# An FNet and GEGLU kernel: a row tile's products a and b taken as 512 and 384 columns instead of 448 and 448

## The chip, the cores and the metric

The kernel runs on one core of a Trainium2 chip. The metric is the device time of one execution in microseconds, as a median over runs. TensorE (PE in the profile; PEld is its loading of weights) multiplies into PSUM, a memory of eight banks of 128 partitions x 512 float32 values. VectorE (DVE) and ScalarE (ACT) read those banks and work on SBUF. GpSimd (POOL) adds some tiles and issues DMAs, and SyncE (SP) issues most DMAs. Each engine works through its own queue in order, and waits for the others by semaphores.

## What is computed

`x` has 2048 rows of 448 values. After a layer norm the kernel takes a two-dimensional Fourier transform of it, real part only, as matrix products, and multiplies it by a gate from a GEGLU block:

```python
a = jnp.einsum("bsd,ed->bse", x, dft_hid_re)
b = jnp.einsum("bsd,ed->bse", x, dft_hid_im)
y = jnp.einsum("ts,bse->bte", dft_seq_re, a) - jnp.einsum("ts,bse->bte", dft_seq_im, b)

def _B_ref(x, w_gate, w_up, w_down):
    return (_gelu(x @ w_gate) * (x @ w_up)) @ w_down

xn = _layernorm(x, axis=-1)
s = _A_ref(xn, A_dft_seq_re, A_dft_seq_im, A_dft_hid_re, A_dft_hid_im)
g = _silu(_B_ref(xn, B_w_gate, B_w_up, B_w_down))
return x + s * g
```

All matrices are float32.

## The kernel before

Each factor of a product is split into a high part, rounded by a ScalarE copy to the type that TensorE takes, and a low part, the rest, by a VectorE subtraction (`split`, L148 to L150: the two lines show as L149 and L150 wherever it is used). A product is then high x high + high x low + low x high.

The program has three stages one after the other. First come the layer norm, the transposes and the GEGLU block (to about 396 us). Then comes the stage of a and b (396 to 477 us), which the change touches. Last comes the transform along the sequence (477 us to the end), which uses a and b. The order of every instruction is the order in which the code is written; nothing is rescheduled. The framework adds the waits, and it treats the accesses of two engines to one PSUM tile as ordered.

**The stage of a and b** is the loop at L1213 over 16 row tiles k of 128 rows, in the order 0 to 13, 15, 14. In a row tile `hid_mm` (L1095) makes two products, each of 11 matmuls (4 high x high, 3 high x low, 4 low x high) into one PSUM bank: `ab{k}_0` is a, 448 columns, and `ab{k}_1` is b, 448 columns. The rows of x in high and low part (`xth`, `xtl`) are the weights, and the two transform matrices along the hidden axis are the moving operand. Those are prepared by `e_split` (L955) in four tiles of 128 contraction rows, the matrices side by side, 896 columns.

Two kinds of row tile follow.
- Row tiles 10 and 15 (`KP`) go to `hid_plain` (L1109). ScalarE and VectorE split a (L149, L150), then minus b (L1112, L1113).
- The other 14 go to `hid_sums` (L1118). ScalarE copies a into pieces 0 and 7 of a buffer `f`, 224 columns each (L1123), and minus b into pieces 2 and 6 (L1124). VectorE makes four more pieces of them (L1129 to L1132). A row tile later `hid_split` (L1136) splits the seven pieces (ScalarE L1141, VectorE L1144). From row tile 2 on there are two buffers `f` in turn, so L1123 of a row tile waits for L1144 of the tile two before it. From k = 11 the split stands right behind the sums.

In row tiles 2 to 5 ScalarE also does a SiLU (L1239). Ahead of the first three row tiles and between them a few products of the block before (`po`, L422) are sent.

**The stage behind it** runs over units of one row tile each (`seven`, L1282): seven products in seven banks, each a matmul of 448 columns with the high part of the factors (L1289) and one of 224 columns with the low part (L1292). `sum_c` (VectorE, L1194 and L1195) and `prep_c` (ScalarE L149, then VectorE L150) prepare the factors of a unit. Those of unit 0 are prepared in row tile 10, and those of units 1 to 3 right behind the loop: `prep_c(1)`, then the sums of row tile 14, then `prep_c(2)` and `prep_c(3)` (L1253 to L1256). The place that `prep_c(1)` writes held the hidden matrices, so it waits for the last matmul of row tile 14. The banks of the seven products are those of the last row tiles of the stage before, in turn: 11, 12, 13, 15 and 14.

Of the kernel before, what the change touches and what calls it, by code (L numbers as in the profile page):

```python
# [8 lines left out]
F32 = mybir.dt.float32  # L9
FR = mybir.dt.float32r  # L10
AF = mybir.ActivationFunctionType
ALU = mybir.AluOpType
# [3 lines left out]
D = 448  # L16
# [11 lines left out]
HD = D // 2  # L28
# [31 lines left out]
def fnet_geglu(ctx: ExitStack, tc: tile.TileContext, xw, ca, ct, cp, et, wss, wd, out):  # L60
# [15 lines left out]
    nc = tc.nc  # L76
# [24 lines left out]
    a_ws = sb.tile([P, 7680], FR, name="w")  # L101
# [12 lines left out]
    def part(t, off, a, b):  # L114
        v = t[:, off : off + a * b].rearrange("p (a b) -> p a b", a=a)
        return v
# [4 lines left out]
    xth = [part(a_x[c], 0, 4, 512) for c in range(NC)]  # L121
    xtl = [part(a_x[c], 2048, 4, 512) for c in range(NC)]
# [5 lines left out]
    def bank(i, name):  # L128
        return psum.tile([P, 512], F32, name=name, tag=f"b{i}")
# [3 lines left out]
    def in_turn(kind, name):  # L133

        first, n = {"mm": (0, 4), "tp": (4, 2), "o": (6, 2), "x": (0, 5), "po": (5, 3), "all": (0, 8)}[kind]
        turns[kind] += 1
        return bank(first + turns[kind] % n, name)
# [10 lines left out]
    def split(h, l, src):  # L148
        nc.scalar.activation(h, src, AF.Copy)  # L149
        nc.vector.tensor_sub(l, src, h)  # L150
# [400 lines left out]
    with tc.manual_schedule():  # L551
# [356 lines left out]
        h, l = [[v[:, n] for n in range(4)] for v in (xth[1], xtl[1])]  # L908
# [21 lines left out]
        e_raw, e_at = {}, {}  # L930
# [24 lines left out]
        def e_split(b):  # L955

            r = e_raw[b]
            if b == 3:
                e_at[b] = []
                for i in range(2):  # L960
                    h, q = a_ws[:, 3584 + i * D :][:, :D], r[:, i * D : (i + 1) * D]
                    nc.scalar.activation(h, q, AF.Copy)
                    nc.vector.tensor_sub(h[64:], q[64:], h[64:].bitcast(F32))
                    e_at[b].append(h)
                return
            v = (a_ws[:, 1792:3584], a_d[1], a_ws[:, :1792])[b]
            split(v[:, : 2 * D], v[:, 2 * D :], r)
            e_at[b] = [v[:, i * D : (i + 1) * D] for i in range(4)]

        for n, (p, f) in enumerate(blocks):  # L970
            g = f // 2
# [9 lines left out]
            if p == 0:  # L981
# [12 lines left out]
                if f in (8, 11):  # L994

                    k = slice(0, 4, 3) if f == 8 else slice(1, 3)
                    for i in range(2):
                        v, w = [u[:, i * 2048 :][:, :2048] for u in (sp, a_x[1].bitcast(F32))]
                        v, w = [u.rearrange("p (k d) -> p k d", k=4)[:, k] for u in (v, w)]
                        nc.sync.dma_start(v, w)  # L1000
            elif f == 2:
                q = None
                for v, w in zip(prep, t1_steps[6][1:]):
                    v.append(w)
                dn[3] = then(send, *t1_steps[7][:2])
            elif f == 3:

                late = then(late[0], t1_steps[7][2]), late[1]
                v = sb.tile([P, 8 * D], F32, name="gacc2", tag="u1")
                for c in range(2):  # L1010
                    gacc[2 + c] = part(v, c * 4 * D, 4, D)
                    nc.sync.dma_start(v[:, c * 4 * D :][:, : 4 * D], gsp[c])
                v = sb.tile([P, 4096], FR, name="w2", tag="u0")
                slots.append((v[:, :WH], v[:, WH : WH + WL]))
            elif f == NF - 3:
                e_load(2)
            elif f == NF - 2:
                dn[1] = dn[3] = then(send, send)
                prep[2].append(lambda: e_split(2))
                prep[2].extend([lambda b=b: e_load(b) for b in (1, 0, 3)])  # L1020
            elif f == NF - 1:
                prep[1].append(lambda: e_split(0))
                prep[2].extend([lambda: e_split(3), lambda: e_split(1)])
                dn = [then(send, send), send, nop, nop]
# [56 lines left out]
        def f_at(k):  # L1081
            if k == 1:
                return a_t[:, : 8 * HD]
            if k % 2 == 0 and k < 13:
                return a_r[:, : 8 * HD]
            if "d0" not in new:
                new["d0"] = sb.tile([P, 4 * D], F32, name="f1", tag="d0")
            return new["d0"]

        TS, ab, behind = {}, {}, []  # L1090
# [4 lines left out]
        def hid_mm(k):  # L1095
            c, kk = divmod(k, 4)
            sl = slice(kk * P, (kk + 1) * P)
            ps = []
            for r in range(2):
                p = in_turn("x" if k < 2 else "all", f"ab{k}_{r}")  # L1100
                mm = [(xth[c][:, b, sl], e_at[b][r]) for b in range(4)]
                mm += [(xth[c][:, b, sl], e_at[b][2 + r]) for b in range(3)]
                mm += [(xtl[c][:, b, sl], e_at[b][r]) for b in range(4)]
                for n, (a, b) in enumerate(mm):
                    nc.tensor.matmul(p[:, :D], a, b, start=n == 0, stop=n == len(mm) - 1)  # L1105
                ps.append(p[:, :D])
            return ps

        def hid_plain(k, ps, spots):  # L1109
            split(spots[0][:, :D], spots[0][:, D:], ps[0])  # L1110
            h, l = spots[1][:, :D], spots[1][:, D:]
            nc.scalar.activation(h, ps[1], AF.Copy, scale=-1.0)  # L1112
            nc.vector.scalar_tensor_tensor(  # L1113
                l, ps[1], -1.0, h.bitcast(F32), op0=ALU.mult, op1=ALU.subtract
            )
            ab[k] = [(v[:, :D], v[:, D:]) for v in spots]

        def hid_sums(k, ps):  # L1118


            fs[k] = f_at(k)
            f = fs[k].rearrange("p (i d) -> p i d", d=HD)
            nc.scalar.activation(f[:, 0:8:7], ps[0].rearrange("p (i d) -> p i d", i=2), AF.Copy)  # L1123
            nc.scalar.activation(  # L1124
                f[:, 2:7:4], ps[1].rearrange("p (i d) -> p i d", i=2), AF.Copy, scale=-1.0
            )

            def sums_():
                nc.vector.tensor_sub(f[:, 4], f[:, 7], f[:, 0])  # L1129
                nc.vector.tensor_sub(f[:, 3], f[:, 6], f[:, 7])  # L1130
                nc.vector.tensor_sub(f[:, 5], f[:, 6], f[:, 4])
                nc.vector.tensor_sub(f[:, 1], f[:, 2], f[:, 5])  # L1132

            return sums_
# [77 lines left out]
        nc.sync.dma_start(a_x[1].bitcast(F32), sp)  # L1212
        for k in [*range(14), 15, 14]:  # L1213
            ps = hid_mm(k)
            if k == 0:
                late[0]()
# [6 lines left out]
            if k in KP:  # L1223
                hid_plain(k, ps, [rest(v) for v in ((new["u0"], new["u1"]), a_x[1:3])[k > 10]])
            else:
                hid_sums(k, ps)()
# [9 lines left out]
            if 2 <= k < 6:  # L1236

                c = k - 2
# [13 lines left out]
        load_c(5)  # L1252
        prep_c(1)  # L1253
        sums14 = hid_sums(14, ps)
        prep_c(2)
        prep_c(3)  # L1256
# [87 lines left out]
        for m, (j, k) in enumerate(units):  # L1344
            u = m % UN
            end = j == NK // 2 - 1
            if u == 0:
                ps = {q: bank(banks[i], f"p{q}_{j}") for i, q in enumerate(PRODUCTS)}
            if k in KS:
# [7 lines left out]
                for i in range(8):  # L1357
                    if u != at[i]:
                        continue
                    i, h = divmod(i, 4)  # L1360
                    TS[KX[(j + 1) % 2][i]] = TS[KX[j % 2][i]]
                    n = KX[(j + 1) % 2][i]
                    a, b = [v.rearrange("p (b d) -> p b d", d=D) for v in (TS[n], td[n])]
                    a, b = a[:, PARTS[h]], b[:, PARTS[h]]
# [135 lines left out]
```

## Time and profile before

| | |
|---|---|
| median of 3 runs | 768.38 us (768.17 to 768.41) |
| the profiled execution's own time | 768.08 us |
| its span, first to last instruction | 766.3 us |
| matmuls | 4041, of them 352 in the stage of a and b |
| granted TensorE clock | 0.999 |

Rows of the profile read as: line, engine, operation, out<-in by the program's names (x rows<-row type), count | busy us, mean ns of one | idle us before, and who ended it. Rows of a timeline begin with the start and the duration in us from the span's start, and end, in brackets, with the engine's idle time before the instruction and who ended it. The matmul's own duration (365 ns for 448 columns) holds its way through the array; the next one starts well before it ends, so the time of a step is read from one start to the next.

### The profile page before, as it was taken

The numbers are of one execution on the slowest core, as the hardware profiler recorded it, in microseconds if no ns is written. First come the engines' busy times: TensorE is split into PE (matmuls) and PEld (weight loads), VectorE is DVE, ScalarE is ACT, GpSimd is POOL, SyncE is SP. The second block draws the span as 40 slices with busy tenths as digits, with TensorE's granted clock in tenths as the row PEclk, the third lists the DMA queues.
The fourth block names the chain that finished last, engine by engine and source line by source line (L and its number), as shares of the span: only waits on it lengthen the run. The fifth ranks groups of instructions, "written<-read, shape, count | busy, mean of one in ns | idle before, by whom it ended". The sixth has DMA issues, their size and how long they took to land.

```text
span 766.3 us, 11490 instructions
## 1 busy us (share of the span) xinstructions
PE 760.0 (99%) x4041; PEld 685.6 (89%) x4041; DVE 641.7 (84%) x1087; ACT 351.4 (46%) x499; POOL 122.8 (16%) x162
## 2 busy tenths in 40 slices
PE   9999999999999999999999999999999999999997
PEld 8988888888888888888889999999999999999997
DVE  7987789999989888988876677988889797979786
ACT  5866433444435334343344755544444344444441
POOL 2002332422434224232200000000000000000000
PEclk9999999999999999999999999999999999999999
DMA  8077484949568563738642732869696969788794
GB/s 299 15 223 233 118 246 138 233 154 243 205 142 298 139 207 82 223 79 245 153 184 85 296 165 69 279 224 338 209 352 206 341 213 311 248 279 277 246 324 153
DMA packets 81034, 162.28 MB, mean 212 GB/s; under 512 B 8016, under 2 KB 62800, under 8 KB 79568
## 3 DMA queue, kind: packets, MB, share of 16 engines
q1 hardware_dynamic: 75648, 135.02, 51.5%
q0 software_dynamic: 5184, 26.41, 16.1%
q8 instruction: 32, 0.52, 0.3%
q14 instruction: 26, 0.21, 0.1%
q10 hardware_dynamic: 144, 0.11, 0.0%
HBM read 139.36 MB, written 51.25 MB: 249 GB/s over the span
## 4 chain that ended last, share of the span: by engine, by line
PE 98%; DVE 1%; issue 0%; ACT 0%; DVEq 0%
PE x L444 24%; PE p L1289 21%; PE po L422 18%; PE p L1292 10%; PE ab L1105 9%; PE x L456 4%; PE gu L371 3%; PE gu L592 2%; PE py L1309 1%; PE py L1311 1%; PE py L1310 1%; PE pt L206 1%; PE warm L571 1%; PE pt L649 0%; DVE cc L1384 0%
## 5 line engine op out<-in xcount | busy, mean ns | idle before, releaser
L422 PE MATMUL po<-wd,hs 128*128 128x448 f32 x672 | 152.7, 366 | 0.0
L422 PEld LDWEIGHTS po<-wd,hs 128*128 128x128 f32 x672 | 125.8, 188 | 14.2
L444 PE MATMUL x<-xt,w 128*128 128x512 f32 x432 | 114.1, 391 | 0.0
L444 PEld LDWEIGHTS x<-xt,w 128*128 128x128 f32 x432 | 81.1, 188 | 15.3
L149 ACT ACTIVATE w<-raw 128x896 fp32r<-128x896 f32 (+1 forms) x59 | 53.6, 910 | 61.9 <-DVE raw L1195 22.4
L444 PE MATMUL x<-t,w 128*128 128x512 f32 x276 | 80.8, 391 | 0.0
L433 DVE TENSOR_TENSOR gacc<-gacc,po 128x448 f32<-128x448 f32 x96 | 58.5, 615 | 14.3 <-PE po L422 14.2
L1105 PE MATMUL ab<-w,xt 128*128 128x448 f32 x256 | 68.1, 365 | 0.0
L521 ACT ACTIVATE hs<-tmp 128x512 fp32r<-128x512 f32 x24 | 15.2, 633 | 101.1 <-DVE tmp L519 101.1
L444 PEld LDWEIGHTS x<-t,w 128*128 128x128 f32 x276 | 51.8, 188 | 9.3
L1289 PE MATMUL p<-xt,w 128*128 128x448 f32 x168 | 54.3, 374 | 0.0
L320 POOL TENSOR_TENSOR raw<-raw 128x256 f32<-128x256 f32 x23 | 19.7, 858 | 212.0 <-DMA raw<-wss 158.2
L1334 POOL DMA_DIRECT2D cc<-xw x14 | 12.3, 881 | 252.8 <-DVE raw L1194 96.1
L1105 PEld LDWEIGHTS ab<-w,xt 128*128 128x128 f32 x256 | 48.1, 188 | 3.8
L149 ACT ACTIVATE w<-f 128x896 fp32r<-128x896 f32 (+1 forms) x34 | 30.2, 888 | 41.7 <-DVE f L1195 17.4
L150 DVE TENSOR_TENSOR w<-raw,w 128x896 fp32r<-128x896 f32 (+1 forms) x40 | 41.8, 1046 | 2.0 <-ACT w L149 1.4
L339 ACT ACTIVATE w<-raw 128x768 fp32r<-128x768 f32 x24 | 20.3, 846 | 39.8 <-POOL raw L326 39.8
L1289 PE MATMUL p<-ts_g,w 128*128 128x448 f32 x112 | 36.3, 374 | 0.0
L1289 PE MATMUL p<-ts_u,ts_tmp 128*128 128x448 f32 x112 | 36.3, 374 | 0.0
L1289 PE MATMUL p<-hs,w 128*128 128x448 f32 x112 | 35.5, 374 | 0.0
L1105 PE MATMUL ab<-wd,xt 128*128 128x448 f32 x96 | 35.1, 365 | 0.0
L1289 PEld LDWEIGHTS p<-xt,w 128*128 128x128 f32 x168 | 31.5, 188 | 2.4
(297 smaller groups left out, 1849.6 us busy)
## 6 DMA issues: line engine op xcount, KB each, us to landing
sums<-ca SPq DMA_DIRECT2D x16, 896.0 KB, 8.8
sums<-ca POOLq DMA_DIRECT2D x16, 896.0 KB, 9.8
raw<-ct SPq DMA_DIRECT2D x69, 192.0 KB, 4.2
raw<-wss SPq DMA_DIRECT2D x24, 512.0 KB, 3.8
ts_u<-td SPq DMA_DIRECT2D x24, 448.0 KB, 5.7
ts_g<-td SPq DMA_DIRECT2D x24, 448.0 KB, 6.5
raw<-sums SPq DMA_DIRECT2D x69, 128.0 KB, 4.1
f<-ct SPq DMA_DIRECT2D x39, 192.0 KB, 4.5
```

Source lines behind the costliest of these rows:

```text
L149: nc.scalar.activation(h, src, AF.Copy)
L150: nc.vector.tensor_sub(l, src, h)
L320: eng.tensor_add(r[:, 1:16:14], r[:, 0:14:13], r[:, 9:17:7])
L339: nc.scalar.activation(h[:, :n], src[:, :n], AF.Copy)
L371: nc.tensor.matmul(ps[:, cols], a, xt[:, k, cols], start=n == 0, stop=n == len(mm) - 1)
L422: nc.tensor.matmul(po[:, :D], hs[:, a, kk * P : (kk + 1) * P], wdn[:, b, i], start=n == 0, stop=n == 5,)
L433: nc.vector.tensor_add(ga, ga, po[:, :D])
L444: nc.tensor.matmul(ps, a[i], b[j], start=first and n == 0, stop=n == 2, skip_group_check=True)
L456: nc.tensor.matmul(ps, a[0], x_, start=False, stop=True, skip_group_check=True)
L1105: nc.tensor.matmul(p[:, :D], a, b, start=n == 0, stop=n == len(mm) - 1)
L1289: nc.tensor.matmul(ps[q][:, :D], h, v, start=u % UN == 0, stop=False, skip_group_check=True)
L1292: nc.tensor.matmul(ps[q][:, :HD], l, v[:, :HD], start=False, stop=u % UN == NS - 1, skip_group_check=True,)
```

## The change

The two products of a row tile are cut at another column. a and b stand side by side, 896 columns; the first bank now takes columns 0 to 511 (all of a and the first 64 of b), the second bank the other 384 of b. What reads b reads it in pieces: in `hid_plain` 64 and 384 columns, in `hid_sums` 64, 160 and 224. Lines move by up to three: L1105 becomes L1104, L1124 becomes L1129, L1129 to L1132 become L1132 to L1135, L1141 and L1144 become L1144 and L1147, L1194 and L1195 become L1197 and L1198, L1289 and L1292 become L1292 and L1295.

```diff
--- before.py
+++ after.py
@@ -956,16 +956,15 @@
 
             r = e_raw[b]
             if b == 3:
-                e_at[b] = []
+                e_at[b] = [a_ws[:, 3584 : 3584 + 2 * D]]
                 for i in range(2):
                     h, q = a_ws[:, 3584 + i * D :][:, :D], r[:, i * D : (i + 1) * D]
                     nc.scalar.activation(h, q, AF.Copy)
                     nc.vector.tensor_sub(h[64:], q[64:], h[64:].bitcast(F32))
-                    e_at[b].append(h)
                 return
             v = (a_ws[:, 1792:3584], a_d[1], a_ws[:, :1792])[b]
             split(v[:, : 2 * D], v[:, 2 * D :], r)
-            e_at[b] = [v[:, i * D : (i + 1) * D] for i in range(4)]
+            e_at[b] = [v[:, : 2 * D], v[:, 2 * D :]]
 
         for n, (p, f) in enumerate(blocks):
             g = f // 2
@@ -1096,23 +1095,24 @@
             c, kk = divmod(k, 4)
             sl = slice(kk * P, (kk + 1) * P)
             ps = []
-            for r in range(2):
-                p = in_turn("x" if k < 2 else "all", f"ab{k}_{r}")
-                mm = [(xth[c][:, b, sl], e_at[b][r]) for b in range(4)]
-                mm += [(xth[c][:, b, sl], e_at[b][2 + r]) for b in range(3)]
-                mm += [(xtl[c][:, b, sl], e_at[b][r]) for b in range(4)]
+            for r, cols in enumerate((slice(0, 512), slice(512, 2 * D))):
+                p = in_turn("x" if k < 2 else "all", f"ab{k}_{r}")[:, : cols.stop - cols.start]
+                mm = [(xth[c][:, b, sl], e_at[b][0]) for b in range(4)]
+                mm += [(xth[c][:, b, sl], e_at[b][1]) for b in range(3)]
+                mm += [(xtl[c][:, b, sl], e_at[b][0]) for b in range(4)]
                 for n, (a, b) in enumerate(mm):
-                    nc.tensor.matmul(p[:, :D], a, b, start=n == 0, stop=n == len(mm) - 1)
-                ps.append(p[:, :D])
-            return ps
+                    nc.tensor.matmul(p, a, b[:, cols], start=n == 0, stop=n == len(mm) - 1)
+                ps.append(p)
+            return ps[0][:, :D], (ps[0][:, D:], ps[1])
 
         def hid_plain(k, ps, spots):
             split(spots[0][:, :D], spots[0][:, D:], ps[0])
             h, l = spots[1][:, :D], spots[1][:, D:]
-            nc.scalar.activation(h, ps[1], AF.Copy, scale=-1.0)
-            nc.vector.scalar_tensor_tensor(
-                l, ps[1], -1.0, h.bitcast(F32), op0=ALU.mult, op1=ALU.subtract
-            )
+            for cols, v in zip((slice(0, 512 - D), slice(512 - D, D)), ps[1]):
+                nc.scalar.activation(h[:, cols], v, AF.Copy, scale=-1.0)
+                nc.vector.scalar_tensor_tensor(
+                    l[:, cols], v, -1.0, h[:, cols].bitcast(F32), op0=ALU.mult, op1=ALU.subtract
+                )
             ab[k] = [(v[:, :D], v[:, D:]) for v in spots]
 
         def hid_sums(k, ps):
@@ -1121,9 +1121,12 @@
             fs[k] = f_at(k)
             f = fs[k].rearrange("p (i d) -> p i d", d=HD)
             nc.scalar.activation(f[:, 0:8:7], ps[0].rearrange("p (i d) -> p i d", i=2), AF.Copy)
-            nc.scalar.activation(
-                f[:, 2:7:4], ps[1].rearrange("p (i d) -> p i d", i=2), AF.Copy, scale=-1.0
-            )
+            b0, b1 = ps[1]
+            n = 512 - D
+            for to, v in (
+                (f[:, 2, :n], b0), (f[:, 2, n:], b1[:, : HD - n]), (f[:, 6], b1[:, HD - n :])
+            ):
+                nc.scalar.activation(to, v, AF.Copy, scale=-1.0)
 
             def sums_():
                 nc.vector.tensor_sub(f[:, 4], f[:, 7], f[:, 0])
```

On ScalarE, at the end of the stage, before (ab_0_3911 and ab_1_3923 are a and b of row tile 15, ab_0_3943 and ab_1_3955 those of tile 14, w<-raw the high parts of units 1 and 2; the semaphores that a row waits for stand in brackets):

```order
L1141 ACTIVATE hs_77<-f_3559 128x7x224 [waits DVE_49,Activation_49]
L149 ACTIVATE xt_67<-ab_0_3911 128x448 [waits PE_49]
L1112 ACTIVATE xt_68<-ab_1_3923 128x448 [waits PE_49]
L149 ACTIVATE w<-raw 128x896 [waits DMAHW1_49,DMAHW2_49,DVE_49,PE_49]
L1123 ACTIVATE f_3559<-ab_0_3943 128x2x224 [waits Activation_49]
L1124 ACTIVATE f_3559<-ab_1_3955 128x2x224 [waits PE_49]
L149 ACTIVATE w<-raw 128x896 [waits DMAHW4_49,DMAHW3_49,Pool_49]
```

The same place in the change (ab_0_3939 and ab_1_3951 are the 512 and the 384 columns of row tile 15, ab_0_3973 and ab_1_3985 those of tile 14):

```order
L1144 ACTIVATE hs_77<-f_3565 128x7x224 [waits DVE_49,Activation_49]
L149 ACTIVATE xt_67<-ab_0_3939 128x448 [waits PE_49]
L1112 ACTIVATE xt_68<-ab_0_3939 128x64 [waits DVE_49]
L1112 ACTIVATE xt_68<-ab_1_3951 128x384 [waits PE_49]
L149 ACTIVATE w<-raw 128x896 [waits DMAHW2_49,DMAHW1_49,PE_49]
L1123 ACTIVATE f_3565<-ab_0_3973 128x2x224 [waits Activation_49]
L1129 ACTIVATE f_3565<-ab_0_3973 128x64
L1129 ACTIVATE f_3565<-ab_1_3985 128x160 [waits PE_49]
L1129 ACTIVATE f_3565<-ab_1_3985 128x224
L149 ACTIVATE w<-raw 128x896 [waits DMAHW4_49,DMAHW3_49,Pool_49]
```

One read of b has become two in row tile 15 and three in row tile 14. The 64-column read of tile 15 waits for VectorE where its forerunner waited for TensorE: for VectorE's L150 below, which reads the same bank. On VectorE the same place in the change reads:

```order
L1147 TENSOR_TENSOR hs_77<-f_3565,hs_77 128x7x224 [waits Activation_49]
L1197 TENSOR_TENSOR raw<-raw 128x128 [waits DMAHW2_49,DMAHW1_49]
L1198 TENSOR_TENSOR raw<-raw 128x128 [waits DVE_49]
L150 TENSOR_TENSOR xt_67<-ab_0_3939,xt_67 128x448 [waits Activation_49]
L1113 SCALAR_TENSOR_TENSOR xt_68<-ab_0_3939,xt_68 128x64 [waits Activation_49]
L1113 SCALAR_TENSOR_TENSOR xt_68<-ab_1_3951,xt_68 128x384 [waits Activation_49]
L150 TENSOR_TENSOR w<-raw,w 128x896 [waits DVE_49,Activation_49]
```

Before, one L1113 of 448 columns stood there in place of two; the rows around it are the same. TensorE's matmuls keep their order; 28 of its groups now also wait for a result of TensorE itself, that of the product which had the bank before.

## The prediction

> **What bounds the kernel now.** I read the page first, then the waits of TensorE, then the stretch from 395 to 480 us in the timeline, where the change sits.
>
> ```profile
> span 766.3 us, 11490 instructions
> PE 760.0 (99%) x4041; PEld 685.6 (89%) x4041; DVE 641.7 (84%) x1087; ACT 351.4 (46%) x499; POOL 122.8 (16%) x162
> PE 98%; DVE 1%; issue 0%; ACT 0%; DVEq 0%
> L1105 PE MATMUL ab<-w,xt 128*128 128x448 f32 x256 | 68.1, 365 | 0.0
> PE warm L571 <- DVE epst L560: 1.1, 1, 1.1
> PE pt L649 <- issue: 0.5, 1, 0.5
> PE gu L592 <- ACT xt L669: 0.2, 1, 0.2
> ```
>
> The page gives TensorE 99% of the span and 98% of the chain that ended last. The last three rows are all of its named waits, and all lie in the first 30 us. A "busy" matmul is not one at full rate, but the kernel's time is still the sum of TensorE's steps from one start to the next. Whatever shortens a step, or stalls TensorE, moves the end one for one. The stage of a and b is 16 row tiles of 22 matmuls (L1105). So there are two questions: what a row tile now takes on TensorE, and whether ScalarE and VectorE still hand over in time.
>
> **Part 1, the matmuls.** The change removes 352 steps of 448 columns and adds 176 of 512 and 176 of 384. Weights, order and columns in sum are the same. From the timeline of TensorE:
>
> ```profile
> 13.10 5.52 PE L592 MATMUL gu<-xt,w 128*128 128x256 f32 x44
> 18.46 0.27 PE L206 MATMUL pt<-ident,xr 128*128 128x128 f32 x1
> 60.04 5.03 PE L422 MATMUL po<-wd,hs 128*128 128x448 f32 x24
> 64.90 5.18 PE L371 MATMUL gu<-xt,w 128*128 128x512 f32 x22
> 69.92 0.84 PE L444 MATMUL x<-xt,w 128*128 128x512 f32 x3
> 71.05 0.84 PE L444 MATMUL x<-t,w 128*128 128x512 f32 x3
> 71.73 0.84 PE L444 MATMUL x<-tq,w 128*128 128x512 f32 x3
> 499.63 0.37 PE L1289 MATMUL p<-hs,w 128*128 128x448 f32 x1
> 501.82 0.38 PE L1289 MATMUL p<-xt,w 128*128 128x448 f32 x1
> ```
>
> From one group's start to the next: 24 steps of 448 columns take 64.90 - 60.04 = 4.86 us, 202.5 ns each. Three of 512 take 0.68 us once settled (71.05 to 71.73), 226.7 ns each. The 22 that follow the 448s take 5.02 us, 228.2 ns each, so going over to 512 costs 22 x 1.5 = 0.03 us once. Those of 256 columns take 5.36 / 44 = 121.8 ns with a slow first one, so I put them at 120. The line through 256 and 512 gives 0.417 ns a column, 173.3 ns at 384, but 200 at 448: the 448s lie 2.5 ns above it. That excess is what the change can save.
>
> No row shows 384 columns. Low bound: the line, 173.3 ns. A row tile is then 11 x 226.7 + 11 x 173.3 + 0.02 to 0.03 us for going over = 4.42 us, against 22 x 202.5 = 4.455 now: 0.035 us saved. High bound from the nearest rows: the pair of a 448 and a 224 (seven pairs from 499.63 to 501.82, 313 ns) lies 6 ns above the line. With 6 ns on each 384 the row tile is 0.03 us longer. With the 2.5 ns of the 448s it saves about 0.01. I take 0.02 us saved in a row tile, 0.3 us over 16, with -0.5 to +0.6 as ends.
>
> The Trainium skill has a rule against this gain: "TensorE: Matmul & The Clock Gate", section "Back-to-back issue gap", puts a warm step at N/2.4 + 2.5 ns, by which 512 + 384 and 448 + 448 cost the same. The 202.5 and 226.7 ns above lie over its 189 and 216, and not by the same amount, so the rows decide; by the rule, part 1 would be zero and the forecast 0.2 us later.
>
> **Part 2, the reads of the products in the 14 row tiles with sums.** One read of 448 columns (L1124) becomes three, of 64, 160 and 224.
>
> ```profile
> 441.54 0.55 ACT L1124 ACTIVATE f<-ab 128x448 f32<-128x448 f32 x1
> 441.98 1.51 ACT L1141 ACTIVATE ts_g<-raw 128x1568 fp32r<-128x1568 f32 x1
> 443.51 1.79 DVE L1144 TENSOR_TENSOR ts_g<-raw,ts_g 128x1568 fp32r<-128x1568 f32 x1 [0.28 <-ACT ts_g L1141]
> 445.40 0.55 ACT L1123 ACTIVATE raw<-ab 128x448 f32<-128x448 f32 x1 [1.92 <-DVE ts_g L1144]
> 445.99 0.55 ACT L1124 ACTIVATE raw<-ab 128x448 f32<-128x448 f32 x1
> L149 ACT ACTIVATE w<-raw 128x896 fp32r<-128x896 f32 x51 | 48.5, 954 | 54.0 <-DVE raw L1195 22.4 <-PE p L1289 12.6 <-PE p L1292 12.5
> ```
>
> From 448 to 896 columns a read grows from 550 to 954 ns: 0.9 ns a column, some 0.15 us fixed. One read starts 0.44 us after the one before (441.54 to 441.98), 0.11 us ahead of its end. So a 64-column read lasts about 0.21 us and holds the queue for 0.11; 160 and 224 together hold it 0.45 against 0.44 now. In a row tile the loop is L1124, L1141, L1144, then L1123 of the next (3.86 us, 441.54 to 445.40), then L1124 again. L1124 could start at 445.40 + 0.42 = 445.82 and starts at 445.99, because it waits for its product: 0.17 us of slack. The 64-column read takes 0.11 of it, the split 0.01, and the shorter row tile 0.02. The loop stays just inside TensorE's pace. I take 0.05 us of delay at the end of this, with 0 and 1.0 as ends (second rival).
>
> **Part 3, row tile 15, the term that decides.** In row tiles 10 and 15 the second product is read by ScalarE (L1112) and VectorE (L1113). Its first 64 columns now share a bank with the first product, and the order shows the 64-column read waiting for VectorE: for the subtraction that reads the first product (L150).
>
> ```profile
> 474.22 0.53 ACT L149 ACTIVATE xt<-ab 128x448 fp32r<-128x448 f32 x1
> 474.64 0.54 ACT L1112 ACTIVATE xt<-ab 128x448 fp32r<-128x448 f32 x1
> 474.35 1.79 DVE L1144 TENSOR_TENSOR hs<-f,hs 128x1568 fp32r<-128x1568 f32 x1 [1.64 <-ACT hs L1141]
> 477.07 0.61 DVE L150 TENSOR_TENSOR xt<-ab,xt 128x448 fp32r<-128x448 f32 x1
> 477.23 0.95 ACT L149 ACTIVATE w<-raw 128x896 fp32r<-128x896 f32 x1 [2.05 <-PE ab L1105]
> 477.61 0.61 DVE L1113 SCALAR_TENSOR_TENSOR xt<-ab,xt 128x448 fp32r<-128x448 f32 x1
> 478.22 1.09 DVE L150 TENSOR_TENSOR w<-raw,w 128x896 fp32r<-128x896 f32 x1
> 479.41 0.33 PE L1292 MATMUL p<-ts_g,w 128*128 128x224 f32 x1
> 479.58 0.37 PE L1289 MATMUL p<-ts_g,w 128*128 128x448 f32 x1
> ```
>
> Now ScalarE is done with tile 15 at 475.18 and idle until 477.23. Behind L1112 in its queue stands the copy of the next stage's factors (L149 at 477.23, unit 1); VectorE subtracts from that at 478.22; TensorE's first low part of unit 1 (479.41) waits for the result. It is already late there: 170 ns to the next start instead of about 100. VectorE is busy without a break from 474.35 to 479.31, so nothing here has slack.
>
> With the wait: subtraction ends 477.07 + 0.61 = 477.68; to ScalarE 0.10 (445.30 to 445.40); the 64-column read holds the queue 0.11, that of 384 0.42 - 0.05 = 0.37; the copy starts at 478.26 and takes 0.95; 0.02 to VectorE; 1.09 for the subtraction; 0.10 to TensorE (479.31 to 479.41). That is 480.42, 1.01 us later than now. A second road ends at the same place: the sixth and seventh products of unit 0 need the banks of tiles 15 and 14, whose last reads now end near 478.95 and 479.78, so unit 1 starts near 480.2. The price lies between 0.8 (small reads overlap more) and 1.3 us.
>
> What comes ahead of this chain moves it. It goes back without a gap to tile 10:
>
> ```profile
> 454.14 0.62 DVE L150 TENSOR_TENSOR ts_u<-ab,ts_u 128x448 fp32r<-128x448 f32 x1
> 455.35 1.51 ACT L1141 ACTIVATE w<-f 128x1568 fp32r<-128x1568 f32 x1
> ```
>
> There the same wait is nearly free: the subtraction ends at 454.76, the 64-column read starts at 454.86, that of 384 at 454.97, and L1141 at 455.34, as now. The chain hangs on TensorE's tiles 0 to 9, which end 10 x 0.02 = 0.2 us sooner.
>
> **Edits that cost nothing.** Reading tile b = 3 of the weights as one view makes the first 512-column step wait for both halves, done before 395.3, while the stage starts at 395.9. The 28 added waits of TensorE for its own results, two or more row tiles back, are met long before; a met wait of this kind stands now at 419.9 us and no gap shows there. If each cost its 51 ns the sum would be 1.4 us.
>
> ```profile
> L1105 PEldq EVENT_SEMAPHORE  x1: 51/51/51, 419.9 to 419.9; - x1
> ```
>
> **Sum.** 1.01 (tile 15) - 0.20 (tiles 0 to 9) + 0.05 (reads) + 0.05 (the second subtraction of tiles 10 and 15 in two pieces, for its fixed part) = +0.91 us. What TensorE gains in tiles 10 to 15 it loses waiting at unit 1. After that it is TensorE-bound again: unit 2 needs its low part at about 482.6, which VectorE has by 482.2. The profiled execution took 768.08 us, its span plus 1.78; 766.3 + 0.91 + 1.78 = 769.0. The median of the runs is 0.30 above that execution, so 769.3 us.
>
> **Rivals.**
> 1. Not slower: the 64-column read's wait is met early, or costs ScalarE nothing, so part 3 falls away and part 1 stays. Place: L1112 of tile 15. It decides if VectorE has subtracted by 475.2. For it: ScalarE has 2 us idle there. Against: VectorE's row at 474.35. Price -0.2 to -0.6: 767.9 to 768.2.
> 2. ScalarE and VectorE become the bound in tiles 4 to 9. A tiny ScalarE instruction holds its queue 0.20 us:
>
> ```profile
> 19.02 0.30 ACT L178 ACTIVATE sd<-mv,epst 128x2 f32<-128x2 f32 x1
> 19.22 1.07 ACT L211 ACTIVATE xt<-pt 128x512 fp32r<-128x512 f32 x2
> ```
>
> If each small read does so too, the loop grows by 0.2 to 0.3 against 0.17 of slack, 0.1 us in each of six tiles; tile 10 passes it on through the new wait, and the second read of tile 15 adds 0.1. 769.3 + 0.7 = 770.0. It decides from 0.16 us of turn for 64 columns.
> 3. Steps of 384 columns cost 6 ns or more above the line. At 6 ns: tiles 0 to 9 bring +0.3 in place of -0.2: 769.8. If they were no quicker than 448 (202.5 ns), 16 x 11 x 29 ns = 5 us: 773. Against that: 256 columns at 120 ns.
>
> **How the numbers follow.** Forecast 0.66, rivals 0.06, 0.17 and 0.11. The forecast's own range, from the ends of parts 1 and 3, is 768.8 to 769.9. 0.2% is 1.54 us, about what a measurement of this kernel can tell from no change; slower by more begins at 769.92. Slower: 0.13 of rival 2, 0.08 of rival 3, and 0.07 of the forecast with every term at its high end, 0.28 together. Faster by as much needs more than all of part 1: 0.02. The rest, 0.70, is within. The range reaches over rivals 2 and 3 near 770 and leaves out rival 1 and the far end of 3: 768.5 to 770.4.
>
> **What would show it.** Right: row tiles 4.42 to 4.45 us apart; L1112 with 64 columns in tile 15 idle about 3 us before it, by VectorE's L150; TensorE idle about 1 us near 478 to 480.4, nowhere else. Wrong: row tiles above 4.46 (part 1); ScalarE's reads of tiles 6 to 9 starting ever later after their products (part 2); or no idle time of TensorE before unit 1 (part 3).

## The result, and the profile after

| | before | after |
|---|---|---|
| median | 768.37 us (767.96 to 768.99, 21 runs) | 769.58 us (769.17 to 770.13, 21 runs) |
| profiled execution, its span | 768.08 us, 766.3 us | 769.64 us, 767.8 us |
| stage of a and b, first step to first step of unit 0 | 81.07 us | 81.35 us |
| idle time of TensorE at units 0 and 1 | 0.06 us | 0.97 us |

The change makes the kernel 1.21 us slower: a ratio of 1.0016, with a 95% interval of 1.0010 to 1.0023. "Idle" here and below is the sum, over the starts of matmuls from 60 us to the end, of what a step takes above its own length by more than 20 ns. All of it lies at units 0 and 1 in both kernels.

From the page of after, the rows that answer to those of before: the span, the engines, the chain that ended last, and the two halves of the stage's matmuls under one heading.

```profile
span 767.8 us, 11550 instructions
PE 761.5 (99%) x4041; PEld 684.2 (89%) x4041; DVE 642.0 (84%) x1089; ACT 352.8 (46%) x529; POOL 123.2 (16%) x162
PE 91%; DVE 4%; ACT 4%; issue 1%; DVEq 0%; ACTq 0%
L1104 PE MATMUL ab<-w,xt 128*128 128x512 f32 (+1 forms) x256 | 68.0, 364 | 0.0
```

TensorE still reads 99%. What changed is the chain: it was 98% TensorE and is 91%. This must be read with care. 8% of the span on VectorE and ScalarE is about 60 us, and not 60 us lost. The chain is followed back from the one place where TensorE waited, and from there it runs along the other two engines through much of the stage of a and b. Lost is only what TensorE stood still at that place, plus what its steps grew. Both have to be measured on TensorE itself.

**The steps.** The timeline of TensorE in one row tile, after first, then before. A row with the weights `wd` starts with the second matmul of a piece, so from one such row to the same row of the next tile is a row tile.

```profile
437.67 0.40 PE L1104 MATMUL ab<-wd,xt 128*128 128x512 f32 x1
437.90 0.85 PE L1104 MATMUL ab<-w,xt 128*128 128x512 f32 x3
438.60 0.40 PE L1104 MATMUL ab<-wd,xt 128*128 128x512 f32 x1
440.15 0.34 PE L1104 MATMUL ab<-wd,xt 128*128 128x384 f32 x1
442.14 0.40 PE L1104 MATMUL ab<-wd,xt 128*128 128x512 f32 x1
```

```profile
437.08 0.36 PE L1105 MATMUL ab<-wd,xt 128*128 128x448 f32 x1
441.54 0.36 PE L1105 MATMUL ab<-wd,xt 128*128 128x448 f32 x1
```

442.14 - 437.67 = 4.47 us after, 441.54 - 437.08 = 4.46 before. To the nanosecond the records have 4.467 and 4.459 on the mean. A row tile got no shorter. The three steps of 512 from 437.90 on show why: to the nanosecond they take 0.693 us, 231 ns each, where settled ones take 226.7. Step by step, from one start to the next in the row tile behind this one (k = 8, from 441.91 us), in ns:

```
512 columns, after 384: 230 233 236 224 231 236 228 232 231 227 227   sum 2535, 11 x 226.7 = 2494
384 columns, after 512: 170 175 178 185 176 181 174 173 173 174 173   sum 1932, 11 x 173.3 = 1906
```

Both sizes end where the line of the prediction puts them, 226.7 and 173.3. But it takes nine steps to get there on the way up and six on the way down, and a row tile pays for both: 41 ns up, 26 down.

The row tiles are not all of the stage's 0.28 us. By the records its 352 matmuls take 71.340 us before and 71.444 after, 0.10 more. The other 0.18 us lies in the 48 matmuls of `po` between the first row tiles, which the change does not touch: 9.727 us before, 9.902 after. The first group of 18 and the row tile behind it, before and then after:

```profile
400.40 3.81 PE L422 MATMUL po<-wd,hs 128*128 128x448 f32 x18
404.05 0.36 PE L1105 MATMUL ab<-w,xt 128*128 128x448 f32 x1
```

```profile
400.72 3.88 PE L422 MATMUL po<-wd,hs 128*128 128x448 f32 x18
404.44 0.40 PE L1104 MATMUL ab<-w,xt 128*128 128x512 f32 x1
```

From start to start that is 3.648 us before, 202.7 ns a step, and 3.714 after, 206.3 ns. Ahead of the group TensorE ran 448 columns before, and runs 384 after.

**The wait in row tile 15.** The timeline of after, ScalarE, VectorE and TensorE:

```profile
474.89 1.79 DVE L1147 TENSOR_TENSOR hs<-f,hs 128x1568 fp32r<-128x1568 f32 x1 [1.64 <-ACT hs L1144]
477.61 0.61 DVE L150 TENSOR_TENSOR xt<-ab,xt 128x448 fp32r<-128x448 f32 x1
478.25 0.61 ACT L1112 ACTIVATE xt<-ab 128x64 fp32r<-128x64 f32 x2 [2.97 <-DVE xt L150]
478.51 0.22 DVE L1113 SCALAR_TENSOR_TENSOR xt<-ab,xt 128x64 fp32r<-128x64 f32 x1 [0.29 <-ACT xt L1112]
478.74 0.96 ACT L149 ACTIVATE w<-raw 128x896 fp32r<-128x896 f32 x1
478.89 0.56 DVE L1113 SCALAR_TENSOR_TENSOR xt<-ab,xt 128x384 fp32r<-128x384 f32 x1 [0.16 <-ACT xt L1112]
479.16 0.27 PE L1295 MATMUL p<-ts_u,xt 128*128 128x224 f32 x1
479.50 0.19 PEld L1292 LDWEIGHTS p<-ts_u,ts_tmp 128*128 128x128 f32 x1 [0.36 <-DVE xt L1113]
479.50 0.47 PE L1292 MATMUL p<-ts_u,ts_tmp 128*128 128x448 f32 x1
479.73 1.09 DVE L150 TENSOR_TENSOR w<-raw,w 128x896 fp32r<-128x896 f32 x1 [0.28 <-ACT w L149]
479.81 0.27 PE L1295 MATMUL p<-ts_u,xt 128*128 128x224 f32 x1
480.30 0.47 PE L1292 MATMUL p<-ts_u,ts_tmp 128*128 128x448 f32 x1 [0.22 <-ACT f L1129]
480.91 0.33 PE L1295 MATMUL p<-ts_g,w 128*128 128x224 f32 x1
```

ScalarE stands idle for 2.97 us, until VectorE has subtracted (477.61 + 0.61 = 478.22). Its copy of unit 1's factors then starts at 478.74, VectorE's subtraction from it at 479.73, and TensorE's first low part of unit 1 at 480.91. From the end of L150 to that start it is 2.69 us; before it was 479.41 - 477.68 = 1.73. So the wait, with the reads and the subtraction in pieces behind it, costs 0.96. TensorE's losses are seen between its starts: 479.16 to 479.50 is some 240 ns more than a 224-column step takes there, 479.81 to 480.30 some 380 ns more. The steps that come late, at 479.50 and 480.30, are the first of the sixth and of the seventh product of unit 0, which wait for their banks: the weight load at 479.50 is released by VectorE's L1113, the matmul at 480.30 by ScalarE's L1129. Each of these two steps then takes 0.10 us longer itself. What is left of the 0.97 is 0.07 at 478.88 and 0.07 at 480.91, the low part of unit 1, where as much was lost before. So the loss shows almost wholly at the banks. The low part, ready at 479.73 + 1.09 = 480.82, would have held TensorE to about the same place without them. Both roads hang on the one wait, and no run here parts them.

The two losses agree with the medians: 0.28 us in the stage, 0.97 - 0.06 = 0.91 us of idle time, 1.19 together, and 1.21 measured. The span grew by 1.5 us because this execution was also 0.36 us later where the stage starts; no instruction is changed ahead of that, and the executions below start the stage between 396.10 and 396.47 us.

### The profile page after: what moved, and what is told of

Same layout as the page of the kernel before. It is cut to its first block, busy times and chain, and to the rows that moved or that the text cites. A ratio compares the mean times of both kernels' runs of the same rounds, so it can differ in the third digit from the quotient of the medians.

```text
span 767.8 us, 11550 instructions
## 1 busy us (share of the span) xinstructions
PE 761.5 (99%) x4041; PEld 684.2 (89%) x4041; DVE 642.0 (84%) x1089; ACT 352.8 (46%) x529; POOL 123.2 (16%) x162
## 4 chain that ended last, share of the span: by engine, by line
PE 91%; DVE 4%; ACT 4%; issue 1%; DVEq 0%; ACTq 0%
PE x L444 24%; PE p L1292 21%; PE po L422 18%; PE p L1295 10%; PE x L456 4%; PE gu L371 3%; PE ab L1104 2%; PE gu L592 2%; PE py L1312 1%; PE py L1314 1%; PE py L1313 1%; PE pt L206 1%; PE warm L571 1%; DVE xt L1147 1%; ACT xt L1144 1%
## 5 line engine op out<-in xcount | busy, mean ns | idle before, releaser
L1104 PE MATMUL ab<-w,xt 128*128 128x512 f32 (+1 forms) x256 | 68.0, 364 | 0.0
L1292 PE MATMUL p<-xt,w 128*128 128x448 f32 x168 | 54.3, 374 | 0.0
L1104 PEld LDWEIGHTS ab<-w,xt 128*128 128x128 f32 x256 | 47.2, 188 | 5.7
L149 ACT ACTIVATE w<-f 128x896 fp32r<-128x896 f32 (+1 forms) x34 | 30.2, 888 | 40.9 <-DVE f L1198 13.4
L150 DVE TENSOR_TENSOR w<-raw,w 128x896 fp32r<-128x896 f32 (+1 forms) x40 | 41.6, 1045 | 1.6 <-ACT w L149 1.0
L1197 DVE TENSOR_TENSOR raw<-raw 128x128 f32<-128x128 f32 x68 | 19.8, 291 | 20.6 <-DMA raw<-sums 20.5
L1292 PE MATMUL p<-ts_u,ts_tmp 128*128 128x448 f32 x112 | 36.6, 376 | 0.3 <-ACT f L1129 0.2
L1292 PE MATMUL p<-ts_g,w 128*128 128x448 f32 x112 | 36.3, 374 | 0.0
L1292 PE MATMUL p<-hs,w 128*128 128x448 f32 x112 | 35.6, 374 | 0.0
L1104 PE MATMUL ab<-wd,xt 128*128 128x512 f32 (+1 forms) x96 | 35.2, 367 | 0.0
```

The lines of the kernel that those rows point to most:

```text
L1104: nc.tensor.matmul(p, a, b[:, cols], start=n == 0, stop=n == len(mm) - 1)
L1197: eng.tensor_add(s2, cr1, s1)
L1292: nc.tensor.matmul(ps[q][:, :D], h, v, start=u % UN == 0, stop=False, skip_group_check=True)
```

## The experiments

For all of them one table: the median with the ratio to before and its interval (the last was run once), the length of the stage, and TensorE's idle time. Of the changed kernels the first four stand against the 27 runs of before, the last two against the 15.

| kernel | median, us | ratio to before | stage, us | idle, us |
|---|---|---|---|---|
| before (27 and 15 runs) | 768.34, 768.40 | | 81.07 | 0.06 |
| ScalarE's copies first | 768.60 | 1.0003 (0.9994 to 1.0012) | 81.35 | 0 |
| row tiles 10 and 15 alone | 769.30 | 1.0013 (1.0004 to 1.0022) | 81.41 | 0.65 |
| the other 14 alone | 768.77 | 1.0007 (0.9999 to 1.0016) | 81.51 | 0 |
| 512 and 384 in turn, step by step | 771.47 | 1.0041 (1.0028 to 1.0053) | 82.50 | 1.74 |
| copies first, every other row tile turned | 768.10 | 0.9997 (0.9988 to 1.0006) | 80.81 | 0.16 |
| other sizes in ten row tiles | 768.6 | one run | 81.34 | 0 |

### ScalarE's copies ahead of VectorE's subtractions

```diff
         def hid_plain(k, ps, spots):
-            split(spots[0][:, :D], spots[0][:, D:], ps[0])
             h, l = spots[1][:, :D], spots[1][:, D:]
-            for cols, v in zip((slice(0, 512 - D), slice(512 - D, D)), ps[1]):
+            spl = list(zip((slice(0, 512 - D), slice(512 - D, D)), ps[1]))
+            nc.scalar.activation(spots[0][:, :D], ps[0], AF.Copy)
+            for cols, v in spl:
                 nc.scalar.activation(h[:, cols], v, AF.Copy, scale=-1.0)
+            nc.vector.tensor_sub(spots[0][:, D:], ps[0], spots[0][:, :D])
+            for cols, v in spl:
                 nc.vector.scalar_tensor_tensor(
```

> The change, but in row tiles 10 and 15 ScalarE's three copies (448, 64 and 384 columns) are issued ahead of VectorE's three subtractions, so that the 64-column copy has no subtraction ahead of it on its bank. Theory (the wait of that copy is 0.96 us of the change's 1.2, the rest is settling of TensorE after a change of columns): TensorE's idle time near 478 to 481 us falls from about 0.97 to 0.1 to 0.3 us (VectorE still does the second subtraction in two pieces), the stage of a and b still takes 0.28 us more than before, the time is 768.6 to 768.8, ratio to before 1.0003 to 1.0006. Rival (the wait lies beside other work, and the steps and small reads cost it): 769.4 to 769.6, idle time unchanged.

Measured: 768.60 us, the stage 81.35 us, and no step of TensorE more than 20 ns over its length after 60 us. The timeline of this kernel at the same place (its lines are shifted: L1111 and L1113 are ScalarE's copies, L1114 and L1116 VectorE's subtractions):

```profile
474.78 0.53 ACT L1111 ACTIVATE xt<-ab 128x448 fp32r<-128x448 f32 x1
475.20 0.59 ACT L1113 ACTIVATE xt<-ab 128x64 fp32r<-128x64 f32 x2
477.62 0.61 DVE L1114 TENSOR_TENSOR xt<-ab,xt 128x448 fp32r<-128x448 f32 x1
477.78 0.95 ACT L149 ACTIVATE w<-raw 128x896 fp32r<-128x896 f32 x1 [1.98 <-PE ab L1104]
478.15 0.67 DVE L1116 SCALAR_TENSOR_TENSOR xt<-ab,xt 128x64 fp32r<-128x64 f32 x2
478.77 1.09 DVE L150 TENSOR_TENSOR w<-raw,w 128x896 fp32r<-128x896 f32 x1
480.05 0.27 PE L1298 MATMUL p<-ts_g,w 128*128 128x224 f32 x1
```

Same reads, same instructions, another order. ScalarE is done with all of b at 475.79, the factors of unit 1 are copied 0.96 us sooner (477.78 for 478.74), and VectorE finishes at 479.86, ahead of TensorE's step at 480.05. By the medians the wait was 769.58 - 768.60 = 0.98 us of the 1.21. The intervals of the two ratios (1.0010 to 1.0023, and 0.9994 to 1.0012) still overlap a little, so the traces carry this: with the stage at 81.35 us in both kernels, the idle time goes from 0.97 to 0. That is less than the 0.1 to 0.3 expected. The rest, 0.2 to 0.3 us, is the stage's 0.28, and this median and the stage's length agree on it. The rival, by which the steps and reads cost it all, falls.

### Row tiles 10 and 15 alone

```diff
-            for r, cols in enumerate((slice(0, 512), slice(512, 2 * D))):
+            n0 = 512 if k in KP else D
+            for r, cols in enumerate((slice(0, n0), slice(n0, 2 * D))):
```

(and where b is read, as before for the 448 and 448).

> 512 and 384 columns in row tiles 10 and 15 alone, 448 and 448 in the other 14. Theory: nearly the whole wait stays (0.8 to 1.0 us of idle time of TensorE near 478 to 481), and settling in two row tiles alone (0.03 us): 769.2 to 769.4. Rival (wait hidden): 768.3 to 768.5.

Measured: 769.30 us, as expected, but not in the expected parts: two misses cancel. TensorE's idle time is 0.65 us, below the 0.8 to 1.0, and the stage is 0.35 us longer where 0.03 was expected. The timeline of TensorE shows it in row tiles 11 to 13, which have 448 columns as before, behind one tile of 512 and 384:

```profile
457.71 0.37 PE L1105 MATMUL ab<-wd,xt 128*128 128x448 f32 x1
462.26 0.37 PE L1105 MATMUL ab<-wd,xt 128*128 128x448 f32 x1
466.80 0.37 PE L1105 MATMUL ab<-wd,xt 128*128 128x448 f32 x1
```

Two row tiles, 44 steps, take 9.09 us: 206.6 ns a step. The same instructions took 202.7 before, and 202.7 still in row tiles 3 to 9 of this kernel. Steps of 448 columns have two settled paces, and which of them holds depends on what ran before. The kept traces say what: between 60 us and unit 0, in every kernel here, each group of 448 columns right behind 512 goes at 202 to 203 ns a step, and each behind a run of eleven 384s at 206 to 207. The `po` groups of the change are three of the latter. Only behind a single 384, in the kernel with the columns in turn below, do both occur. Some 0.08 to 0.09 us is lost in each of the tiles 11, 12, 13 and 14, 0.34 together, and the idle time is 0.32 less than in the change. That fits the step of the prediction by which tile 15's chain hangs on tile 10: what TensorE loses behind tile 10 it doesn't wait at unit 1.

### The 14 others alone

The same edit with `k not in KP`, and `hid_plain` as before.

> 448 and 448 in row tiles 10 and 15, 512 and 384 in the other 14. Theory: no idle time of TensorE at the first units, and the stage of a and b 0.2 to 0.3 us longer than before, since a row tile pays for two changes of columns (41 ns after 384 to 512, 26 ns after 512 to 384 in the profile of the change): 768.5 to 768.7. Rival (what the prediction said of the steps, 0.02 us saved in a row tile): the stage 0.3 us shorter, 768.1.

Measured: 768.77 us, 0.07 above the expected range, no idle time, the stage 0.44 us longer. What the stage lost in the change would be 0.28; the two row tiles of 448 columns, now between others, take 4.54 us each in place of 4.46, which is the rest. This and the first run are two kernels without the wait, and neither is faster than before. So the wait did not hide a gain of the matmuls: there was none.

### 512 and 384 in turn, step by step

```diff
                 for n, (a, b) in enumerate(mm):
-                    nc.tensor.matmul(p, a, b[:, cols], start=n == 0, stop=n == len(mm) - 1)
+                    for p, cols in zip(ps, cuts):
+                        nc.tensor.matmul(p, a, b[:, cols], start=n == 0, stop=n == len(mm) - 1)
```

(the two banks are taken at the start of the row tile).

> The change, but the two products of a row tile are sent together, 512 and 384 columns in turn, so that the columns change at each of the 22 steps and not twice in a row tile. If each change of columns costs 26 to 41 ns: 0.65 us more in a row tile, the stage 10 us longer, 779 to 781. If a step costs what its columns cost whatever came before, and the slow steps after a change are a matter of long runs: a pair takes 226.7 + 173.3 = 400 ns, a row tile 4.40 us, the stage 0.8 to 1.1 us shorter than in the change. There both products are done only at the end of the row tile, so the wait in row tile 15 stays and can grow by some tenths.

Measured: 771.47 us. Neither number came. From the timeline of TensorE, one row tile of 22 steps, and the sixth product of unit 0:

```profile
457.95 0.57 PE L1107 MATMUL ab<-wd,xt 128*128 128x512 f32 x2
462.50 0.57 PE L1107 MATMUL ab<-wd,xt 128*128 128x512 f32 x2
479.76 0.27 PE L1297 MATMUL p<-ts_u,xt 128*128 128x224 f32 x1
480.64 0.44 PE L1294 MATMUL p<-ts_u,ts_tmp 128*128 128x448 f32 x1 [0.61 <-DVE xt L1115]
```

A row tile takes 4.55 us, a pair of steps 413.4 ns: 237.3 and 176.0, which never settle. That is 13.3 ns a pair above the settled 400, not the 67 that two whole settlings would cost, and not nothing. The 41 and 26 ns of a whole settling are spread over nine and six steps; where the next change comes at once, a step of 512 pays 10.6 ns and one of 384 pays 2.7, every time. The stage is 1.15 us longer than in the change and the idle time 0.77 us longer, 1.92 together against 771.47 - 769.58 = 1.89. The second part is the wait again: row tile 15's two products end together at the end of the row tile, so everything behind them starts later.

### Copies first, and every other row tile turned

```diff
-            for r, cols in enumerate((slice(0, 512), slice(512, 2 * D))):
+            cuts = [(0, slice(0, 512)), (1, slice(512, 2 * D))]
+            for r, cols in cuts[::-1] if k % 2 and k < 15 or k == 14 else cuts:
```

(and in `hid_sums` of the turned row tiles the reads of 160 and 224 columns come ahead of those of 448 and 64).

> The change with ScalarE's copies first (as in the run before with that edit), and in every other row tile the product of 384 columns is taken ahead of that of 512, so that TensorE's steps run 22 of one size and then 22 of the other. Theory (a step costs 13.3 ns above N/2.4, plus settling after each change of columns, 41 ns going up and 26 going down, once in a row tile where it was twice): row tiles of 4.40 + 0.034 = 4.43 us on the mean, the stage 0.4 us shorter than before, no idle time of TensorE at the first units, 767.9 to 768.2. Rival (the excess of the change is a cost of each product's start, whatever its columns: new bank, added wait): row tiles stay at 4.467, the stage 0.28 us longer, 768.6.

Measured: 768.10 us. The timeline of TensorE: the second step of a run of 512, of the next run of 384, and of the next run of 512; between them, rows from the settled part of a run of 512 across the border of two row tiles. The last row is a weight load of unit 1.

```profile
456.87 0.40 PE L1105 MATMUL ab<-wd,xt 128*128 128x512 f32 x1
458.49 0.39 PE L1105 MATMUL ab<-wd,xt 128*128 128x512 f32 x1
460.99 0.39 PE L1105 MATMUL ab<-wd,xt 128*128 128x512 f32 x1
461.84 0.34 PE L1105 MATMUL ab<-wd,xt 128*128 128x384 f32 x1
465.73 0.40 PE L1105 MATMUL ab<-wd,xt 128*128 128x512 f32 x1
479.35 0.19 PEld L1302 LDWEIGHTS p<-ts_g,w 128*128 128x128 f32 x1 [0.17 <-DVE w L150]
```

465.73 - 456.87 = 8.86 us for two row tiles, 4.43 each, as expected. In the settled part the 11 steps from 458.49 to 460.99, with the border of two row tiles among them, take 2.50 us, 227 ns each. No step at the start of a product stands out there, though the bank changes at it and the added waits of TensorE for its own results stand at such starts. So the start of a product costs nothing that shows; the change of columns does, and the rival falls. The stage is 0.26 us shorter than before, not 0.4. Its own 352 matmuls do take 0.37 us less (70.97 for 71.34), but the `po` groups between the first row tiles take 0.11 more: two of the three stand behind 384 columns and go at 206 ns a step, the one behind 512 at 202.7. The idle time expected to be nothing is 0.16 us. It lies at the low part of unit 1, which waits for VectorE's L150 as it did before the change. The kernel's median is 0.3 us below before, which its interval (0.9988 to 1.0006) can't tell from no change. Of the kernels run it has the lowest median.

### Other sizes

The cut between the products at 504, 496, 480, 464 or 456 columns in two row tiles each, the rest as in the first experiment.

> The copies-first kernel with the cut between the two products at another column in some row tiles: 504 and 392 columns in tiles 3 and 4, 496 and 400 in 5 and 6, 480 and 416 in 7 and 8, 464 and 432 in 9 and 11, 456 and 440 in 12 and 13, 512 and 384 elsewhere. A probe of what a step of N columns takes once settled. If the line through 256, 384 and 512 holds for all N: 13.3 ns above N/2.4 everywhere, and 448 is the only exception with 15.8. If only multiples of 128 lie on it, the others lie 2 to 7 ns above. The time is within 0.8 us of that of the copies-first kernel, 768.6.

One run: 768.6 us, as expected. Three steps lie between the two rows of each pair below (the timeline of TensorE; 400 columns, and 416 in the two row tiles that have it):

```profile
431.85 0.34 PE L1105 MATMUL ab<-wd,xt 128*128 128x400 f32 x1
432.40 0.34 PE L1105 MATMUL ab<-wd,xt 128*128 128x400 f32 x1
440.74 0.35 PE L1105 MATMUL ab<-wd,xt 128*128 128x416 f32 x1
441.30 0.35 PE L1105 MATMUL ab<-wd,xt 128*128 128x416 f32 x1
445.20 0.35 PE L1105 MATMUL ab<-wd,xt 128*128 128x416 f32 x1
445.77 0.36 PE L1105 MATMUL ab<-wd,xt 128*128 128x416 f32 x1
```

400 columns take 183.3 ns, 16.7 above N/2.4 (the 0.417 ns a column of the prediction's line). 416 take 186.7 in one row tile and 190 in the next: 13.4 above, then 16.7. So the line holds for 384 and 512, others mostly lie above it, and 416 has two paces, as 448 has. Eleven steps are few to call a pace settled; some of the ten pieces still alternate at the end.

## Why the prediction came out

The prediction was 769.3 us with 768.5 to 770.4, no difference of over 0.2% the likeliest case; measured were 769.58 and 0.16%. Its sum was +0.91 us, and the trace of after gives +1.14 once the later start of the stage is taken off (1.50 at the last matmul less 0.36). By its parts:

- **Part 3, row tile 15: right.** The price of the wait was put at 1.01 us plus 0.05 for the second subtraction in two pieces. The chain in the trace holds both: 0.96. Taking the wait away, with every read left in, gave back 0.98. The order of events was the predicted one to a tenth of a microsecond a step: ScalarE idle 2.97 us ("about 3"), and both roads end close together, the banks of unit 0's last products and the low part of unit 1. Rival 1, by which the wait is met early, decides at 475.2; VectorE was done at 478.22.
- **Part 1, the steps: the step that failed, in its sign.** The settled prices were right, 226.7 and 173.3. What was mis-sized is the "0.02 to 0.03 us for going over". It was counted once in a row tile and read from one row, 22 steps of 512 behind 448. It is 0.041 us going up and 0.026 going down, 0.067 together, against the 0.059 that leaving 448 saves (4.459 less 4.400; by the prediction's rows 0.055). In place of 0.02 us saved a row tile lost 0.008 in the settled part of the stage. The first three, with the `po` behind each, lost 0.03 to 0.08. That is `po` at its second pace, 0.18 us of the stage's 0.28 in all, and the prediction had no term for it. The stage changed by +0.28 us where -0.3 stood, inside the ends of -0.5 to +0.6. At tile 15's L150 this shows as +0.18 instead of -0.20 us: 0.38 too low. The rest of the sum, 1.11 for the wait, the reads and the second subtraction, was 0.15 too high, so the error left is 0.23 us. That the two errors have opposite signs is luck.
- **The Trainium skill's rule** ("TensorE: Matmul & The Clock Gate", section "Back-to-back issue gap"), by which 512 + 384 costs what 448 + 448 does, comes nearer than the forecast's part 1: a row tile grew by 0.2% in the settled part. The trace agrees with the equality and not with the rule's terms: the fixed part here is 13.3 ns, not 2.5, and what the 448s lose above it the change pays in settling. The section calls its formula the gap of an isolated matmul, and gives about 131 ns at N = 512 for a sustained stream with weight loads; the stream here settles at 226.7, above both. The turned kernel, at 4.43 us, breaks the equality.
- **Part 2, ScalarE's reads: right, with little to spare.** From the timeline of ScalarE in after:

```profile
437.05 0.55 ACT L1123 ACTIVATE raw<-ab 128x448 f32<-128x448 f32 x1 [0.33 <-DVE ts_u L1147]
437.49 0.70 ACT L1129 ACTIVATE raw<-ab 128x64 f32<-128x64 f32 x3
438.08 1.52 ACT L1144 ACTIVATE ts_g<-f 128x1568 fp32r<-128x1568 f32 x1
441.52 0.55 ACT L1123 ACTIVATE f<-ab 128x448 f32<-128x448 f32 x1 [1.92 <-DVE ts_g L1147]
```

  The loop turns in 441.52 - 437.05 = 4.47 us, TensorE's pace. Within it the 64-column read lasts 0.22 us and holds the queue for 0.15, where 0.21 and 0.11 were taken; behind it at most 0.05 us of slack is left (the same read holds it for 0.10 in row tiles 11 and 12, where the next product is ready). Rival 2 asked for a loop longer than TensorE's; ScalarE's reads start no later after their products from tile to tile.
- **Row tile 10: right.** There the wait costs nothing that reaches TensorE: no step is late between 60 and 478 us.
- **Rival 3** asked for steps of 384 at 6 ns or more above the line. Settled they are on it; over the 11 steps of a product they lie 2.4 ns above.
- **The edits put at nothing: right.** Where the columns do not change, at the borders of row tiles of 512 in the turned kernel, no step stands out at the start of a product.

## What to carry to other kernels

When a tile in PSUM gets readers on two engines, the order in which the reads are written decides who waits: one engine's reads issued together, ahead of the other's, took away a wait of about 1 us here and added no instruction. The Trainium skill ("PSUM — Partial Sum Buffer", section "PSUM bank collisions raise a hardware error") says that the two reads may not simply run at once; no run here shows that, since every kernel kept them in order. Here matmuls of equal length did better in long runs: the stage was 0.28 us longer than before with eleven of a size in a row and 0.26 us shorter with twenty-two. A step's price is not its columns alone. An exchange of sizes that saves a few ns a step must first pay for each change, and it can slow matmuls that nobody touched, as it did `po`. And the share of an engine in the chain that ended last is not the time that it costs: 8% went to VectorE and ScalarE for a loss of under 1 us.

## What was not expected of the hardware

- After a change in the number of columns TensorE needs several steps to settle, nine going up and six going down, in nearly the same pattern each time once the row tiles follow each other: 230, 233, 236, 224, 231, 236, 228, 232, 231, then 227 ns for 512 after 384; 41 ns in all, and 26 ns for 384 after 512.
- The same matmul has two settled paces: 448 columns at 202.7 ns behind 512 columns and, behind a run of 384, at 206.6 ns for three row tiles on end; 416 columns at 186.7 and 190.
- With the columns changing at every step, pairs of 512 and 384 take 413.4 ns and stay there.

What lies behind the two paces, the runs don't say. The loading of weights, which overlaps the matmuls, took 188 ns in each kernel's stage (up to 192 in the one of other sizes) and was not tried apart.
